# A recurrence with an early expert: weight loads issued one per half step behind a small GpSimd copy, masks moved to chunk 16, VectorE's splits put off

## The chip, the core and the metric

The kernel runs on one core of a Trainium2 chip. The metric is the device time of one execution in microseconds (us). Five engines take part: PE (TensorE, with PEld for its weight loads), ACT (ScalarE), DVE (VectorE), POOL (GpSimd) and SP (SyncE, which only issues DMAs). Each has a queue of its own that it works through in order; semaphores tie the queues together. In the profile, q1 is the DMA queue that SyncE and ScalarE feed, q0 the one that GpSimd feeds; both are served by the same 16 DMA engines.

## What is computed

A delta-rule attention without softmax over 768 tokens (4 batches, 8 heads, head size 48), and then a top-1 mixture of 8 experts on its 3072 output rows of 384 columns.

```python
k_n = k / (norm(k) + 1e-6)
for t in range(768):
    y[t]  = q[t] @ state
    v_old = k_n[t] @ state
    state = state + beta[t] * outer(k_n[t], v[t] - v_old)
x = y.reshape(3072, 384)                       # rows (batch, token)
e = argmax(x @ w_gate); gate = softmax(x @ w_gate)[e]
# each expert takes its rows in order, up to a capacity of 768
out[row] = gate * (relu(x[row] @ w1[e]) @ w2[e])
```

## The kernel before

**The recurrence.** The 768 tokens are cut into 24 chunks of 32. Inside a chunk the dependence between tokens is solved beforehand into a small triangular matrix T (`prepare` and `solve`, on VectorE, done by chunk 16), so that chunk c needs, for each half g of the heads (g = 0, 1), these steps in a row:

- `product_k` (line 326, TensorE): k times the state, into the tile ks in PSUM;
- `residual` (line 336, VectorE): R = vs - ks, where vs is v scaled by the norms (`tokens`, line 300, VectorE, for chunk c + 2 at the end of chunk c);
- `update` (lines 347 and 354): u = T times R on TensorE, and four copies of u, 32 partitions each, from PSUM into the tile u in SBUF;
- `state` (lines 367 and 375): the state s grows by k times u on TensorE, and four copies bring it from PSUM into the tile x, from which the next chunk's `product_k` reads.

The two halves run interleaved, so that a chunk is two half steps (c,0) and (c,1). Between them stand the output y of the chunk (lines 383 and 392, copied into xt at line 518, the last one at line 570), its store to xbuf in DRAM, and the logits of the router. `turn` (line 319) loads T for the next chunk as four DMAs of 32 KB from SyncE's queue. The score products P of a chunk pair are masked once on VectorE; `flush` (line 156) issues the masks that are ready, one pair ahead.

**Sharing.** From chunk `SHARED` = 18 on, the second half of the state copies goes to VectorE (line 375), and the router's and the early expert's work is done in the loop itself: after each `update`, `rt.step(budget=630)` issues one stage of the router's chain of small VectorE operations (`route`), `extra` splits weights of the early expert, `grab` issues the gathers of its rows once these are known. In the three half steps of `PARTED` two of the four copies of u are VectorE's as well.

**The early expert.** Expert number 0 in the order of processing is the one that has most rows after chunk 15 (`order`, line 895; its index is the tile widx). Its weights come by five indirect DMAs from GpSimd (`Experts.load`, line 1197): three of 512 KB for w1, two of 768 KB for w2. `LDS` says how many are issued at the head of a chunk: two in chunk 19, one each in 20 to 22. A weight is then split into a high part hw (a rounding copy on ScalarE, line 1056) and a low part lw = rw - hw (line 1057): by GpSimd for w1, by VectorE from chunk 22 on. `PCS` gives the number of these splits per half step; what is left follows behind the loop. The gathered rows are transposed in chunks 21 and 22 (`Experts.turn`, line 972) and split in the same way into x0h and x0l (lines 973 and 974).

**What sets the order.** In the loop the order on every engine is the order in which the code is written. The experts behind it are put in order by a scheduler.

The lines that issue the early weights and the splits:

```python
for _ in range(LDS.get(c, 0)):
    self.ahead.load()
```

## Time and profile before

| what | us |
|---|---|
| median of three executions | 514.58 (514.39 to 516.59) |
| the profiled execution, its own time | 516.29 |
| its span, first to last instruction | 514.5 |

| engine | busy us | share of the span | instructions |
|---|---|---|---|
| PE | 433.9 | 84% | 7404 |
| PEld | 373.3 | 73% | 7404 |
| DVE | 321.0 | 62% | 1043 |
| ACT | 281.1 | 55% | 784 |
| POOL | 121.7 | 24% | 122 |

The shares are means over stages. The recurrence takes about the first half of the span, the experts the second; chunks 16 to 23 lie between 193 and 257 us. In a timeline row stand the start, the duration, the engine, the line, the operation with the tile it writes and those it reads, the shape and how many instructions were merged; in brackets at the end, how long the engine was idle before and who released it ("issue" means that the trace names nobody).

### The profile page before, as it was taken

How to read it: one execution, taken by the hardware profiler on the slowest of the kernel's cores; microseconds unless marked ns; L12 is line 12 of the kernel's file. 1: busy time of each engine (PE TensorE's matmuls, PEld its weight loads, DVE VectorE, ACT ScalarE, POOL GpSimd, SP SyncE). 2: the span in 40 equal slices, each digit the busy share in tenths (PEclk: the TensorE clock that was granted, in tenths of full speed). 3: DMA queues.
4: the chain of work that ended last, by engine and by line, in shares of the span. 5: the costliest groups of instructions: out<-in, count | busy, mean ns of one | idle time of the engine just before them, and what ended most of it. 6: DMA issues, size and time to landing. Idle time of an engine off the chain costs nothing. (4 is left out here: it accounts for less than half of the span.)

```text
span 514.5 us, 17642 instructions
## 1 busy us (share of the span) xinstructions
PE 433.9 (84%) x7404; PEld 373.3 (73%) x7404; DVE 321.0 (62%) x1043; ACT 281.1 (55%) x784; POOL 121.7 (24%) x122
## 2 busy tenths in 40 slices
PE   5835766678888989957799899999999999999990
PEld 3424555456666666745589888999999999999990
DVE  1999699697999993747685736263360817263210
ACT  2237567687778888836652635273562818363210
POOL 6011000000000000226026453434253453521110
PEclk9885678798889999979999999999999999999996
DMA  5977223563335445557118274525144453610000
GB/s 154 236 233 200 60 79 84 175 173 84 91 86 180 103 114 148 152 147 195 44 46 294 90 244 141 164 89 199 72 162 170 154 186 89 205 72 31 29 32 14
DMA packets 49705, 67.17 MB, mean 131 GB/s; under 512 B 29084, under 2 KB 38230, under 8 KB 49619
## 3 DMA queue, kind: packets, MB, share of 16 engines
q0 software_dynamic: 9280, 34.98, 20.4%
q1 hardware_dynamic: 37570, 23.52, 17.8%
q10 hardware_dynamic: 2768, 7.47, 5.2%
q8 instruction: 60, 0.98, 0.8%
q14 instruction: 27, 0.21, 0.1%
HBM read 53.50 MB, written 12.43 MB: 128 GB/s over the span
## 5 line engine op out<-in xcount | busy, mean ns | idle before, releaser
L1098 DVE SCALAR_TENSOR_TENSOR hl<-hp,hh 128x256 fp32r<-128x256 f32 (+7 forms) x64 | 35.5, 554 | 92.1 <-ACT hh L1097 91.8
L1197 POOL DMA_INDIRECT rw<-in_w_dram,widx x40 | 40.9, 1022 | 143.5 <-DVE R L336 115.0
L354 ACT COPY u<-u 32x192 f32<-32x192 f32 x186 | 57.5, 309 | 22.2 <-PE u L347 17.8
L375 ACT COPY x<-s 48x192 f32<-48x192 f32 x164 | 51.3, 313 | 24.3 <-PE s L367 20.0
L1057 DVE TENSOR_TENSOR lw<-rw,hw 128x384 fp32r<-128x384 f32 (+1 forms) x106 | 59.6, 605 | 6.3 <-ACT hw L1056 6.3
L1095 PE MATMUL hp<-xh,hw 128*128 128x444 f32 (+6 forms) x168 | 58.9, 353 | 0.0
L1095 PE MATMUL hp<-xh,lw 128*128 128x444 f32 (+6 forms) x168 | 58.0, 345 | 0.0
L1095 PE MATMUL hp<-xl,hw 128*128 128x444 f32 (+6 forms) x168 | 58.0, 345 | 0.0
L1056 ACT CAST hw<-rw 128x384 fp32r<-128x384 f32 (+1 forms) x112 | 56.5, 557 | 0.1
L240 DVE TENSOR_TENSOR tmp<-M,AT 128x28 f32<-128x28 f32 (+23 forms) x180 | 55.8, 333 | 0.2
L245 DVE TENSOR_TENSOR M<-M,tmp 128x28 f32<-128x28 f32 (+23 forms) x180 | 55.8, 333 | 0.1
L347 PE MATMUL u<-R,T 128*64 128x48 f32 x736 | 35.2, 236 | 23.9 <-DVE R L336 14.4
L1097 ACT ACTIVATE hh<-hp 128x256 fp32r<-128x256 f32 (+7 forms) x64 | 31.3, 490 | 41.2 <-PE hp L1095 40.7
L1139 POOL DMA_INDIRECT out_dram<-ys,dst_row x27 | 29.1, 1078 | 101.6 <-ACT ys L1138 59.9
L347 PEld LDWEIGHTS u<-R,T 128*64 128x64 f32 x736 | 29.0, 147 | 32.7 <-DVE R L336 20.4
L132 PE MATMUL gp<-kq 48*32 48x64 f32 (+1 forms) x1792 | 27.4, 252 | 15.6 <-ACT P L152 6.7
L367 PE MATMUL s<-u,k 64*48 64x96 f32 x736 | 35.2, 271 | 4.6 <-ACT u L354 2.9
L132 PEld LDWEIGHTS gp<-kq 48*32 48x32 f32 x1792 | 21.9, 127 | 22.9 <-issue 8.5
L1115 PE MATMUL yT<-hh,hw 128*128 128x444 f32 (+3 forms) x96 | 34.2, 360 | 0.0
L1115 PE MATMUL yT<-hh,lw 128*128 128x444 f32 (+3 forms) x96 | 33.7, 354 | 0.0
L1115 PE MATMUL yT<-hl,hw 128*128 128x444 f32 (+3 forms) x96 | 33.4, 357 | 0.0
L367 PEld LDWEIGHTS s<-u,k 64*48 64x48 f32 x736 | 21.5, 129 | 15.4 <-ACT u L354 8.5
(219 smaller groups left out, 932.8 us busy)
## 6 DMA issues: line engine op xcount, KB each, us to landing
kq<-in_kqf_dram ACTq DMA_DIRECT2D x12, 448.0 KB
xbuf<-xt SPq DMA_DIRECT2D x24, 192.0 KB
v<-in_vt_dram SPq DMA_DIRECT2D x22, 192.0 KB
k<-in_kt_dram SPq DMA_DIRECT2D x21, 192.0 KB
kq<-in_kqf_dram SPq DMA_DIRECT2D x8, 448.0 KB
mb<-M SPq DMA_DIRECT2D x5, 512.0 KB
T<-mb SPq DMA_DIRECT2D x80, 32.0 KB
kq<-in_kqf_dram SPq DMA_DIRECT2D x4, 224.0 KB
```

Of the source, the lines that this page charges most:

```text
L132: nc.tensor.matmul(gp[a][32 * r : 32 * r + 32, i, t], kq[rows, 0, 4 * t + r], kq[rows, k0:k1, 4 * t + r], start=True, stop=True,)
L240: nc.vector.tensor_tensor(tv, M[:, :, r0:r1, j : j + 1].to_broadcast([128, G, m, n]), AT[:, :, j : j + 1, 32 - n : 32].to_broadcast([128, ...
L245: return lambda: nc.vector.tensor_tensor(v, v, tv, ALU.add)
L347: nc.tensor.matmul(us[p][64 * p : 64 * p + 64, m], T[:, 4 * g + m, 2 * p : 2 * p + 2].rearrange("p a b -> p (a b)"), R[:, m], start=True, ...
L354: copy(U[32 * r : 32 * r + 32, 4 * g : 4 * g + 4, r], us[r // 2][32 * r : 32 * r + 32])
L367: nc.tensor.matmul(self.S[h][64 * a : 64 * a + 48, t], kt[rows, m], U[rows, m, 2 * h : 2 * h + 2], start=first, stop=True, skip_group_chec ...
L375: copy(Xn[rows, ts, 2 * h : 2 * h + 2, a], self.S[h][rows, ts])
L1056: (nc.scalar.copy if e else self.hi)(hi[p], raw[p])
L1057: (nc.vector.tensor_tensor if e else self.lo)(lo[p], raw[p], hi[p], ALU.subtract)
L1095: nc.tensor.matmul(hp, a, b, start=i == 0, stop=i == len(terms) - 1)
L1115: self.nc.tensor.matmul(yT[m], a, b, start=j == 0, stop=j == len(terms) - 1)
L1197: nc.gpsimd.indirect_dma_start(out=raw[:, i * st : i * st + st].rearrange("p k m -> p (k m)"), out_offset=None, in_=tab[:, :], in_offset=b ...
```

## The change

- **Loads.** `LDS` is now a list of five half steps, (19,0), (19,1), (20,0), (20,1) and (21,1). Behind the `update` of each, GpSimd first copies one column of that half step's u into a tile of one column, z, and then issues one load. The copy waits for u, and GpSimd's queue behind it waits too.
- **A new function** `behind` does what followed the update from chunk `SHARED` on: work put off (`pay`), one stage of the router, the load, `grab`, `extra`. The gathers of `grab` now stand ahead of the splits of `extra`.
- **Splits.** In (20,0), (20,1), (21,0) one, two and three splits of w1 are done instead of two each.
- **VectorE's splits put off.** The low parts that VectorE computes in chunks 21 to 23 (x0l, and lw of w2) are kept in a list, `owed`, and issued by `pay` behind the next update.
- **Masks.** In chunk 16 `flush` is called for the last chunk, so that the three masks left are issued there; those of chunks 17, 19 and 21 go.
- **Sharing.** `SHARED` is 17, and in every half step from there on VectorE has one of the four copies of u (two in `PARTED`, as before).

```diff
-LDS = {19: 2, 20: 1, 21: 1, 22: 1}
-PCS = {(20, 0): 2, (20, 1): 2, (21, 0): 2, (22, 0): 1, (23, 0): 1}
+LDS = ((19, 0), (19, 1), (20, 0), (20, 1), (21, 1))
+PCS = {(20, 0): 1, (20, 1): 2, (21, 0): 3, (22, 0): 1, (23, 0): 1}
...
-SHARED = 18
+SHARED = 17
...
-            copy = nc.vector.tensor_copy if (c, g) in PARTED and r > 1 else nc.scalar.copy
+            copy = nc.vector.tensor_copy if c >= SHARED and r > 2 - ((c, g) in PARTED) else nc.scalar.copy
...
     def extra(self, c, i):
-        self.ahead.step(PCS.get((c, i), 0), self.nc.scalar.copy, self.nc.vector.tensor_tensor if c > 21 else None)
+        self.ahead.step(PCS.get((c, i), 0), self.nc.scalar.copy, self.defer if c > 21 else None)
+
+    def defer(self, *args):
+        self.owed.append(args)
+
+    def pay(self):
+        for args in self.owed:
+            self.nc.vector.tensor_tensor(*args)
+        self.owed = []
+
+    def behind(self, c, g):
+
+        self.pay()
+        self.rt.step(budget=630)
+        if (c, g) in LDS:
+            self.nc.gpsimd.tensor_copy(self.z, self.u[c % 2][:, 4 * g, 0, 0:1])
+            self.ahead.load()
+        self.grab(c)
+        self.extra(c, g)
...
-            for _ in range(LDS.get(c, 0)):
-                self.ahead.load()
...
-            self.flush(c)
+            self.flush(c if c < 16 else KC)
...
             if c >= SHARED:
-                rt.step(budget=630)
-                self.extra(c, 0)
-                self.grab(c)
+                self.behind(c, 0)
...
-                self.ahead.turn(c - KC + 3, self.ps)
+                self.ahead.turn(c - KC + 3, self.ps, lo=self.defer)
...
         rt.step()
+        self.pay()
         self.product_p(KC - 1)
...
         nc.scalar.copy(xh, tp)
-        nc.vector.tensor_tensor(xl, tp, xh, ALU.subtract)
+        (lo or nc.vector.tensor_tensor)(xl, tp, xh, ALU.subtract)
```

The second half step calls `behind(c, 1)` in the same way. The order on the engines, before and after, at three places:

GpSimd from the first load of the early expert's weights on, before (rw is the loaded weight, xg the gathered rows):

```order
L1197 DMA rw_4621<-in_w_dram,widx_75 128x1024 x3
L1057 TENSOR_TENSOR lw_4837<-rw_4621,hw_4836 128x512 x2
L963 DMA xg_4842<-xbuf,src_86 128x384 x2
L1057 TENSOR_TENSOR lw_4837<-rw_4621,hw_4836 128x512 x2
L1197 DMA rw_4942<-in_w_dram,widx_75 128x1536
L1057 TENSOR_TENSOR lw_4837<-rw_4621,hw_4836 128x512 x2
L1197 DMA rw_4942<-in_w_dram,widx_75 128x1536
```

GpSimd at the same place, after:

```order
L451 COPY z<-u_105 128x1
L1211 DMA rw_4674<-in_w_dram,widx_75 128x1024
L451 COPY z<-u_105 128x1
L1211 DMA rw_4674<-in_w_dram,widx_75 128x1024
L451 COPY z<-u_104 128x1
L1211 DMA rw_4674<-in_w_dram,widx_75 128x1024
L977 DMA xg_4842<-xbuf,src_86 128x384 x2
L1071 TENSOR_TENSOR lw_4846<-rw_4674,hw_4845 128x512
L451 COPY z<-u_104 128x1
L1211 DMA rw_4911<-in_w_dram,widx_75 128x1536
L1071 TENSOR_TENSOR lw_4846<-rw_4674,hw_4845 128x512 x5
L451 COPY z<-u_105 128x1
```

The three loads of w1 stand apart, each behind a copy; the gathers have moved ahead of all six split products, of which five now stand in one piece.

VectorE from the state copies in half step (21,1) to R of (22,0), before (sm, wv, ex and Eb are the first stage of the router):

```order
L375 COPY x_102<-s_951 48x2x2x48 x2
L698 TENSOR_REDUCE sm<-lg 128x4
L700 TENSOR_TENSOR wv<-lg,sm 128x32
L702 TENSOR_TENSOR wv<-wv,con 128x32
L704 TENSOR_REDUCE sm<-wv 128x4
L706 TENSOR_TENSOR ex<-lg,sm 128x32
L708 TENSOR_TENSOR Eb<-wv,sm 128x32
L974 TENSOR_TENSOR x0l<-tp,x0h 128x384
L300 TENSOR_TENSOR vs<-v,nt 128x384
L336 TENSOR_TENSOR R<-vs,ks 128x192
```

VectorE at the same place, after:

```order
L376 COPY x_102<-s_951 48x2x2x48 x2
L355 COPY u_105<-u 32x4x48
L712 TENSOR_REDUCE sm<-lg 128x4
L714 TENSOR_TENSOR wv<-lg,sm 128x32
L716 TENSOR_TENSOR wv<-wv,con 128x32
L718 TENSOR_REDUCE sm<-wv 128x4
L720 TENSOR_TENSOR ex<-lg,sm 128x32
L722 TENSOR_TENSOR Eb<-wv,sm 128x32
L301 TENSOR_TENSOR vs<-v,nt 128x384
L337 TENSOR_TENSOR R<-vs,ks 128x192
```

A copy of u has come in ahead of the router's stage, and x0l has left its place ahead of vs and R.

VectorE between R of (22,0) and R of (22,1), before:

```order
L336 TENSOR_TENSOR R<-vs,ks 128x192
L375 COPY x_102<-s_951 48x2x2x48 x2
L724 TENSOR_REDUCE sum<-Eb 128x8
L726 TENSOR_TENSOR pe<-Eb,pp 128x32
L728 TENSOR_TENSOR run<-run,sum 128x8
L730 TENSOR_TENSOR V<-Eb,con 128x4x24
L1057 TENSOR_TENSOR lw_5145<-rw_4942,hw_5144 128x384
L336 TENSOR_TENSOR R<-vs,ks 128x192
```

And after:

```order
L337 TENSOR_TENSOR R<-vs,ks 128x192
L376 COPY x_102<-s_951 48x2x2x48 x2
L355 COPY u_104<-u 32x4x48
L443 TENSOR_TENSOR x0l<-tp,x0h 128x384
L738 TENSOR_REDUCE sum<-Eb 128x8
L740 TENSOR_TENSOR pe<-Eb,pp 128x32
L742 TENSOR_TENSOR run<-run,sum 128x8
L744 TENSOR_TENSOR V<-Eb,con 128x4x24
L337 TENSOR_TENSOR R<-vs,ks 128x192
```

The split of w2 (lw) has gone from its place ahead of R to behind the next update, and x0l of chunk 21 stands here instead, behind the copy of u.

## Rows read from the trace of the kernel before

**Rows 1.** Windows: stretch, length, busy us per engine, granted PE clock, DMA share, GB/s.

```profile
core 0: us, PE busy (x) PEld busy (x) DVE busy (x) ACT busy (x) POOL busy (x), PEclk, DMA share, GB/s
...
218.00:226.00 8.00, 2.61 (x59) 2.07 (x50) 1.78 (x5) 1.50 (x5) 0.00 (x0) 0.75 0.77 225
...
258.00:514.00 256.00, 240.33 (x1480) 230.89 (x1479) 114.52 (x266) 112.40 (x243) 92.81 (x92) 0.98 0.37 125
```

**Rows 2.** Timeline: R(18,0), R(19,0), R(20,0), R(20,1) and the u copies behind it.

```profile
205.76 0.35 DVE L336 TENSOR_TENSOR R<-vs,ks 128x192 f32<-128x192 f32 x1 [0.81 <-PE ks L326]
...
212.57 0.35 DVE L336 TENSOR_TENSOR R<-vs,ks 128x192 f32<-128x192 f32 x1
...
218.44 0.35 DVE L336 TENSOR_TENSOR R<-vs,ks 128x192 f32<-128x192 f32 x1
...
229.42 0.34 DVE L336 TENSOR_TENSOR R<-vs,ks 128x192 f32<-128x192 f32 x1
...
230.63 0.75 DVE L354 COPY u<-u 32x192 f32<-32x192 f32 x2 [0.23 <-PE u L347]
```

**Rows 3.** Timeline: the update's matmuls in half step (20,0).

```profile
222.96 0.42 PE L347 MATMUL u<-R,T 128*64 128x48 f32 x2 [4.17 <-issue]
...
224.59 1.06 PE L347 MATMUL u<-R,T 128*64 128x48 f32 x14 [1.22 <-DMA T<-mb]
```

**Rows 4.** Timeline: the first of three weight loads, and T for chunk 20.

```profile
213.09 1.45 POOL L1197 DMA_INDIRECT rw<-in_w_dram,widx  x1 [115.03 <-DVE R L336]
...
213.47 3.53 SPq L319 DMA_DIRECT2D T<-mb  x4
```

**Rows 5.** DMA queues from 216 to 218 us: packets, MB, share of 16 engines.

```profile
q0 software_dynamic: 145, 0.54, 106.7%
q1 hardware_dynamic: 57, 0.02, 4.8%
```

**Rows 6.** Timeline: VectorE and GpSimd in chunks 20 and 21, with one mask before.

```profile
199.33 0.68 DVE L148 TENSOR_TENSOR P<-P,mask 128x512 f32<-128x512 f32 x1
...
226.47 0.35 DVE L767 TENSOR_TENSOR acc<-acc,ip 128x192 f32<-128x192 f32 x1
...
226.99 2.49 POOL L1057 TENSOR_TENSOR lw<-rw,hw 128x512 fp32r<-128x512 f32 x2 [9.95 <-ACT hw L1056]
227.07 1.22 DVE L780 TENSOR_TENSOR o<-o,top 128x16 f32<-128x16 f32 x1
...
228.53 0.98 DVE L771 CAST src<-of 128x2 int32<-128x2 f32 x1
...
230.27 0.97 POOL L963 DMA_INDIRECT xg<-xbuf,src  x1 [0.79 <-issue]
...
231.41 0.56 DVE L300 TENSOR_TENSOR vs<-v,nt 128x384 f32<-128x384 f32 x1
...
232.57 3.30 DVE L148 TENSOR_TENSOR P<-P,mask 128x512 f32<-128x512 f32 x1
...
232.81 2.50 POOL L1057 TENSOR_TENSOR lw<-rw,hw 128x512 fp32r<-128x512 f32 x2
...
235.47 1.24 POOL L1197 DMA_INDIRECT rw<-in_w_dram,widx  x1 [0.16 <-issue]
```

**Rows 7.** Timeline: R(16,1).

```profile
195.70 0.35 DVE L336 TENSOR_TENSOR R<-vs,ks 128x192 f32<-128x192 f32 x1 [1.38 <-PE ks L326]
```

**Rows 8.** Timeline: R(22,0), ks, a split, R(22,1), R(23,0), the last xt.

```profile
241.94 0.35 DVE L336 TENSOR_TENSOR R<-vs,ks 128x192 f32<-128x192 f32 x1
...
244.09 0.56 PE L326 MATMUL ks<-x,kq 112*32 112x96 f32 x16
...
245.10 0.56 DVE L1057 TENSOR_TENSOR lw<-rw,hw 128x384 fp32r<-128x384 f32 x1 [1.33 <-ACT hw L1056]
...
245.57 0.35 DVE L336 TENSOR_TENSOR R<-vs,ks 128x192 f32<-128x192 f32 x1
...
249.63 0.34 DVE L336 TENSOR_TENSOR R<-vs,ks 128x192 f32<-128x192 f32 x1
...
257.28 0.48 ACT L570 COPY xt<-y 128x384 f32<-128x384 f32 x1 [1.06 <-PE y L392]
```

More of the change, by code (lines that the diff above doesn't have):

```diff
@@ L434, in extra @@
     def extra(self, c, i):
-        self.ahead.step(PCS.get((c, i), 0), self.nc.scalar.copy, self.nc.vector.tensor_tensor if c > 21 else None)
+        self.ahead.step(PCS.get((c, i), 0), self.nc.scalar.copy, self.defer if c > 21 else None)
[4 more added lines that the diff above has]
+            self.nc.vector.tensor_tensor(*args)
+        self.owed = []
+    def behind(self, c, g):
[6 more added lines that the diff above has]
+        self.extra(c, g)
     def grab(self, c):
@@ L539, in run_ @@
                 if c >= SHARED:
-                    rt.step(budget=630)
-                    self.extra(c, 1)
-                    self.grab(c)
+                    self.behind(c, 1)
                 self.maybe(c + 1)
@@ L966, in collect, with turn @@
             )
-    def turn(self, i, ps, tag="gp"):
+    def turn(self, i, ps, tag="gp", lo=None):
         nc, xg, (xh, xl) = self.nc, self.xg[:, i], [x[:, i] for x in self.x]
```

## The prediction

> **What bounds the kernel now.** I read first where TensorE, the engine with the most work, is not working. From 258 us to the end it is busy for 240.33 of 256 us [rows 1]; what the change can shorten lies ahead of that, in the recurrence over 24 chunks. There a chunk goes through TensorE, ScalarE and VectorE and back, one half of the heads after the other; I write R(c,g) for the subtraction of VectorE (line 336) that opens half step g of chunk c. R(23,1) is the last of them, and the others are counted back from it. Where all runs well a chunk takes 5.87 us, from R(19,0) to R(20,0), and half a chunk 2.94 [rows 2]. Then two places stick out.
>
> The first is the update of chunk 20. R(20,0) starts at 218.44, but its matmuls wait 4.17 us and then 1.22 more, the second time plainly for the loads of T; they end at 225.65 (224.59 + 1.06), where in the next half step they are done 1.2 us after R (R at 229.42, the copies of their result at 230.63), which here is 219.65: 6.0 us lost [rows 2, 3]. Those four loads of T start at 213.47 on SyncE's queue (q1), beside three loads of the early expert's weights that GpSimd issues from 213.09 on (q0) [rows 4]. From 216 to 218 q0 takes 106.7% of the sixteen engines and q1 4.8% [rows 5]. So the weights hold T back. TensorE, idle so long, has a mean granted clock of 0.75 in that stretch [rows 1], between its two levels, and stays slow a little longer: from the end of the late matmuls to R(20,1) it takes 3.77 us instead of the 1.7 that remain of a half step (2.94 less 1.2): 2.0 us more [rows 2, 3].
>
> The second is VectorE against GpSimd. A mask product that takes 0.68 us alone takes 3.30 at 232.57, beside two products of GpSimd (2.50 us for both), and all that stands behind it on VectorE is 2.6 us late [rows 6]. A small one with both operands in SBUF suffers alike: 16 columns take 1.22 us from 227.07, to just past the end of the first of two GpSimd products that began at 226.99 [rows 6].
>
> **The change part by part**, from R(20,0) = 0 where it matters.
>
> Chunks 16 to 19. Three masks in one place put 3 x 0.68 = 2.04 us on VectorE in chunk 16, against 1.38 us of idle time before R(16,1) [rows 6, 7]; with what else stands there I take 0.4 us lost. Chunks 17 and 18 hand two of four state copies and one of four u copies per half step from ScalarE to VectorE; chunk 18 takes 6.81 us now and 19, where the state copies are shared already, 5.87 [rows 2]. Of 0.94 too much in chunk 18, and as much in 17, I take 1.3 us as won. But the u copy stands ahead of the routing operations on VectorE, and the next R waits behind these in chunks 18 and 19: up to 0.37 us (half of the 0.75 for two [rows 2]) three times, less a mask of 0.68 gone from (19,0); 0.4 us lost. Sum: 0.5 us won, between 1.1 lost and 1.8 won.
>
> Chunks 20 and 21: before, 241.94 - 218.44 = 23.50 us from R(20,0) to R(22,0) [rows 2, 8]. Each weight load now waits on GpSimd for the u of its half step, so load 1 follows u(19,0). A load's data fills the engines 2 to 3 us after its issue (213.09, full by 216) and for some 2 us (0.54 MB of q0 from 216 to 218, where a load is 0.52 MB) [rows 4, 5], so T for chunk 20, issued 0.9 us after R(19,0), is through before load 1. Loads 2 and 3 fall around T for chunk 21, issued at +0.8 and wanted at about +6.4; with 2 us lost to load 2 and a part of that to load 3 it just makes it. Without waits R(22,0) would come at 2 x 5.87 plus about 0.8 for ScalarE's casts: +12.5, a gain of 11.0.
>
> I do not take that, because of the order on GpSimd. Behind the third load now stand the two gathers of the expert's rows, and behind these all six split products. The gathers need the source rows: VectorE's u copies end 1.96 after R (230.63 + 0.75 - 229.42) [rows 2]; the five small operations from acc to the cast took 3.04 (226.47 to 229.51), of which some 1.85 lie in two that GpSimd held, so 1.2; the gather follows 0.76 after the cast (230.27): +3.9. Two gathers take 2.54 (to the product at 232.81): +6.5. The first product, 1.25: +7.7. The fourth load with its small copy, 1.24 and 0.16 (235.31 to 235.47) and 0.2 taken for the copy (no row has it; between 0 and a product's 1.25): +9.3. Five products in a row, 6.25: +15.55 [rows 6]. The casts they need are done on ScalarE by +10. In this train fall, on VectorE, four small products of the routing step of (21,1), from about +11, and then the v scaling (vs, 0.56 alone), all with both operands in SBUF, and R(22,0) stands behind them. Let each small one pass where a GpSimd product ends, and vs at the train's end: R(22,0) at +16.1. If VectorE is held through the whole train, as the mask was through two, the routing's small ones (0.9 for these) follow it too: +17.0; if nothing is held, +12.5. I take 16.1, since the small product of 1.22 us passed at an end and the large mask did not. TensorE then idles some 4 us, and its clock may fall as it did after 6; half of the 2.0 us above: 1.0. Gain: 23.50 - 16.1 - 1.0 = 6.4.
>
> The Trainium skill says of this place (SBUF — State Buffer, Who interferes with whom) that a VectorE instruction with two SBUF inputs contends with a GpSimd instruction that reads SBUF, and whoever issues second is fully blocked. The 3.30 us agree, though the mask, which waited, could by it have passed between the two products. By the rule R(22,0) comes at +16.1, by the mask's row at +17.0.
>
> Chunk 22. A split of VectorE stands ahead of each next R and waits for ScalarE, 1.33 us at 245.10; R(22,1) starts at 245.57 though ks was done at 244.65 (244.09 + 0.56): 0.92 late [rows 8]. Put off by half a step, the splits stand behind the u copy and wait for nothing. I take 0.9 for the first half and, since VectorE's own queue (u copy, split, routing) is then near its limit, 0.5 for the second: 6.3 us where 7.69 stand (241.94 to 249.63), 1.4 won, between 0.5 and 1.8.
>
> Chunk 23 to the last copy xt: 7.65 us now. In (23,1) u copy and split (0.37, 0.56) now stand ahead of the last routing, which waited for TensorE before; against it a split less ahead of R(23,1). I take 0.2 lost, between 0.5 lost and 0.5 won.
>
> From there, 257.2 us remain (514.50 - 257.28), and the chain (last routing, weights of the next expert, gathers) moves as a whole. The order of the first experts differs: four gathers now go ahead of two output scatters, and TensorE transposes all four in a piece. The gathers start earlier by the scatter that stood ahead, the transposes need the last of the four sooner: nothing, within 1.0 either way. Loads 4 and 5 arrive long before the products of expert 0.
>
> **Sum:** 0.5 + 6.4 + 1.4 - 0.2 = 8.1 us. The profiled execution took 516.29 (span 514.50), 1.71 above the median of 514.58; no row says where, so I take the 8.1 from the median: **506.5 us**.
>
> **The rivals.**
> - *GpSimd's train holds nobody.* For: the rows show VectorE held beside two products, none beside five, and whether its small ones slip between is seen once. Against: the long rows above. Gain 0.5 + 11.0 + 1.4 - 0.2 = 12.7: 501.9. Chance 0.22.
> - *The wait for T moves to chunk 21*, held by loads 2 and 3 as chunk 20's was by three. It ends when load 3 is in; then the routing of (21,1) falls behind the train and is not held. With the 6.0 us and the clock's 2.0, R(22,0) at 12.5 + 8.0 = +20.5, gain 3.0 + 1.7 = 4.7: 509.9. For: q1's 4.8%; against: two loads, not three, and about a microsecond without either between them. Chance 0.12.
> - *The weights were not what held T.* For: the longer wait (4.17) has no releaser named. The Trainium skill (DMA: Bandwidth & Descriptors, Queues, rings and completion order) has each engine go round its queues packet by packet, by which q1 would have kept a share; the 4.8% speak against it. If something else held T, the 6.0 us stay and 8.1 - 6.0 = 2.1 are left: 512.5, no difference. Chance 0.07.
> - *Slower: every T meets a load.* With one load per half step, T for chunks 21, 22 and 23 each run into one (loads 2 and 3, 4, 5). If each waits as chunk 20's did, 3 x 6.0 = 18 us go back against the best case: 501.9 + 18 = 519.9. It decides from the point where a load holds q1 for the 5.6 us between T's issue and its use; three loads did, one filled the engines for 2. Chance 0.04.
>
> **How the numbers follow.** My forecast has 0.55. About 0.5% (2.6 us) is what a measurement of this kernel can tell from no change, so faster means below 512.0: 0.55 + 0.22 + 0.12, less a little for their tails: 0.88; within: 0.08; slower: 0.04. The range reaches down to the first rival with chunks 16 to 19 at their better end (501.0) and up past the second with them at the worse (511.0).
>
> **What would show it.** In the changed kernel's trace: no wait at the update of chunk 20; GpSimd's five products in one piece, with VectorE's wv, ex, Eb and vs beside it at a microsecond or more each; 16 to 17 us from R(20,0) to R(22,0), then 6.3 to R(23,0); the stretch after the last xt within 1 us of 257.2. If the second distance is near 12.5, the train was harmless; if the wait sits at chunk 21's update, the loads still collide.

## The result, and the profile after

The changed kernel takes 521.06 us (median, 520.55 to 523.01), the kernel before beside it 514.91: a ratio of 1.0109, 95% interval 1.0076 to 1.0141. It is slower, by some 6 us. The forecast was 506.5 us with a range of 501.0 to 511.0, and slower had a chance of 0.04.

The profiled execution took 521.12 us, its span is 519.3 us. The openings of the half steps on VectorE, R(18,0), R(19,0), R(20,0), R(20,1), R(22,0) and R(23,0), and the last xt on ScalarE, as in [rows 2, 8]:

```profile
205.56 0.35 DVE L337 TENSOR_TENSOR R<-vs,ks 128x192 f32<-128x192 f32 x1
...
213.69 0.34 DVE L337 TENSOR_TENSOR R<-vs,ks 128x192 f32<-128x192 f32 x1
...
221.95 0.35 DVE L337 TENSOR_TENSOR R<-vs,ks 128x192 f32<-128x192 f32 x1
...
228.91 0.35 DVE L337 TENSOR_TENSOR R<-vs,ks 128x192 f32<-128x192 f32 x1 [3.65 <-remote]
...
241.18 0.35 DVE L337 TENSOR_TENSOR R<-vs,ks 128x192 f32<-128x192 f32 x1 [0.28 <-PE s L368]
...
249.69 0.35 DVE L337 TENSOR_TENSOR R<-vs,ks 128x192 f32<-128x192 f32 x1
...
259.54 0.48 ACT L584 COPY xt<-y 128x384 f32<-128x384 f32 x1 [1.06 <-PE y L393]
```

Cut at such rows, the two spans differ so:

| stretch | before, us | changed, us |
|---|---|---|
| start to R(16,0) | 193.17 | 191.26 |
| chunks 16 to 19 | 25.27 | 30.69 |
| chunks 20 and 21 | 23.50 | 19.23 |
| chunk 22 | 7.69 | 8.51 |
| chunk 23 to the last xt | 7.65 | 9.85 |
| from there to the end | 257.2 | 259.8 |

Chunks 20 and 21, the aim of the change, gain 4.3 us. Everything around them loses. Chunk 18 goes from 6.81 to 8.13 us, chunk 19 from 5.87 to 8.26, with neither loads nor splits in the first of them. What a half step there waits for, in the timeline of (18,1), ScalarE and VectorE:

```profile
210.69 0.97 ACT L355 COPY u<-u 32x192 f32<-32x192 f32 x3
...
211.70 0.36 DVE L355 COPY u<-u 32x192 f32<-32x192 f32 x1 [0.97 <-ACT u L355]
...
213.22 0.55 DVE L301 TENSOR_TENSOR vs<-v,nt 128x384 f32<-128x384 f32 x1
213.69 0.34 DVE L337 TENSOR_TENSOR R<-vs,ks 128x192 f32<-128x192 f32 x1
```

VectorE's one copy of u does not run beside ScalarE's three. It starts when the last of them is done and ends at 212.06, where four copies on ScalarE would have ended too. Behind it stand the router's operations, vs and the next R; R has no bracket, so it came straight off a full queue. A bracket of that kind (0.97 to 2.98 us idle, ended by ScalarE's u) stands at each of the eleven half steps from (17,0) on that are not in `PARTED`; about 1 us of it are ScalarE's three copies. Inside, the two pairs run side by side:

```profile
223.20 0.64 ACT L355 COPY u<-u 32x192 f32<-32x192 f32 x2 [1.13 <-PE u L348]
223.28 0.75 DVE L355 COPY u<-u 32x192 f32<-32x192 f32 x2 [0.35 <-PE u L348]
```

The code says which tiles these are. The result of `update` lies in two PSUM tiles, `us[r // 2]`. In `PARTED` ScalarE reads the first and VectorE the second, and TensorE releases both (the brackets above). With one copy for VectorE, quarter 2 goes to ScalarE and quarter 3 to VectorE from the *same* tile, and in the trace it is ScalarE's third copy, done at 211.66, that releases VectorE's. The tile u that both write in SBUF can't be the reason, since they write it side by side in `PARTED`.

The Trainium skill (PSUM — Partial Sum Buffer, PSUM bank collisions raise a hardware error) has two engines collide in one bank where they touch the same 32 partitions, and not where they touch different ones, as these quarters do. The program waits all the same; no run here tried it without.

### The profile page after: what moved, and what is told of

It is laid out like the page before. It is cut to its first block, busy times and chain, and to the rows that moved or that the text cites. A ratio compares the mean times of both kernels' runs of the same rounds, so it can differ in the third digit from the quotient of the medians.

```text
span 519.3 us, 17641 instructions
## 1 busy us (share of the span) xinstructions
PE 436.0 (84%) x7400; PEld 376.2 (72%) x7404; DVE 322.5 (62%) x1058; ACT 276.9 (53%) x769; POOL 121.2 (23%) x127
## 5 line engine op out<-in xcount | busy, mean ns | idle before, releaser
L376 ACT COPY x<-s 48x192 f32<-48x192 f32 x160 | 50.0, 313 | 29.1 <-PE s L368 22.6
L355 ACT COPY u<-u 32x192 f32<-32x192 f32 x175 | 54.1, 309 | 20.9 <-PE u L348 17.1
L1071 DVE TENSOR_TENSOR lw<-rw,hw 128x384 fp32r<-128x384 f32 (+1 forms) x104 | 58.4, 605 | 1.9 <-ACT hw L1070 1.8
L368 PE MATMUL s<-u,k 64*48 64x96 f32 x736 | 33.5, 269 | 4.2 <-ACT u L355 2.1
L327 PE MATMUL ks<-x,kq 112*32 112x96 f32 x736 | 29.0, 272 | 5.3 <-issue 5.3
```

Of the source, the lines that this page charges most:

```text
L355: copy(U[32 * r : 32 * r + 32, 4 * g : 4 * g + 4, r], us[r // 2][32 * r : 32 * r + 32])
L376: copy(Xn[rows, ts, 2 * h : 2 * h + 2, a], self.S[h][rows, ts])
L1071: (nc.vector.tensor_tensor if e else self.lo)(lo[p], raw[p], hi[p], ALU.subtract)
```

## Experiments

Every ratio is taken against runs of the kernel before on the same chip. e1 to e8 ran on one chip (the kernel before: 511.35 and 511.22 us there), e9 to e12 and f1 to f4 on a second (515.22 and 516.10), f5 and f6 on a third (515.08); the chip of the result above is not on record. Stretches in us are read from one profiled execution each, at the rows named above. Executions of one kernel lie up to 8 us apart (e4: 512.28 to 520.34), so a difference of a stretch counts where several kernels show it or a row shows the wait.

| kernel | ratio, 95% interval | 16 to 19 | 20 and 21 | 22 | 23 | behind xt |
|---|---|---|---|---|---|---|
| before | 1 | 25.27 | 23.50 | 7.69 | 7.65 | 257.2 |
| changed, again (e11) | 1.0146, 1.0096 to 1.0196 | 32.19 | 19.33 | 10.18 | 9.86 | 261.4 |
| e1, third quarter | 0.9879, 0.9812 to 0.9946 | 25.89 | 17.01 | 6.49 | 7.88 | 254.6 |
| e2, u as before | 0.9872, 0.9795 to 0.9948 | 25.02 | 18.53 | 8.03 | 7.69 | 255.4 |
| e3, two of four | 0.9966, 0.9928 to 1.0004 | 26.95 | 16.53 | 8.01 | 8.63 | 254.9 |
| e4, before + u copy | 1.0078, 1.0032 to 1.0123 | 30.76 | 17.68 | 8.19 | 9.99 | 255.0 |
| e5, before + pacing | 0.9944, 0.9910 to 0.9977 | 25.19 | 19.66 | 8.13 | 7.65 | 254.5 |
| e6, before + put off | 0.9956, 0.9916 to 0.9996 | 25.27 | 23.15 | 6.67 | 7.69 | 256.3 |
| e7, before + masks, 17 | 0.9938, 0.9898 to 0.9978 | 24.52 | 21.72 | 8.11 | 7.65 | 255.4 |
| e8, e1 + three T | 0.9938, 0.9903 to 0.9973 | 26.59 | 16.56 | 8.26 | 7.87 | 254.6 |
| e9, e1 + short train | 0.9949, 0.9918 to 0.9979 | 26.41 | 17.65 | 6.61 | 9.18 | 258.1 |
| e10, e8 + short train | 1.0000, 0.9972 to 1.0028 | 30.28 | 17.70 | 6.61 | 9.18 | 259.1 |
| e12, before + three T | 0.9984, 0.9949 to 1.0019 | 28.13 | 18.78 | 7.69 | 7.65 | 260.4 |
| f4, e9 + late loads | 0.9938, 0.9910 to 0.9967 | 26.36 | 18.86 | 6.61 | 9.18 | 259.2 |
| f5, f4 + late gathers | 1.0059, 1.0022 to 1.0096 | 26.58 | 21.05 | 7.72 | 9.19 | 260.2 |
| f6, e1 + late gathers | 0.9955, 0.9921 to 0.9988 | 26.64 | 17.76 | 6.50 | 7.87 | 259.4 |

### The copy of u

**e1: VectorE takes the third quarter, ScalarE the fourth.** The same number of copies on each engine; now VectorE's comes first on the shared tile.

```diff
-... c >= SHARED and r > 2 - ((c, g) in PARTED) ...
+... c >= SHARED and r in ((2, 3) if (c, g) in PARTED else (2,)) ...
```

> The changed kernel, only that VectorE copies the third quarter of u and ScalarE the fourth (the number of copies on each engine is the same). In the changed kernel the copy of VectorE starts 1 to 1.9 us late, since ScalarE reads the same PSUM tile ahead of it. Theory A (this wait is the loss): without it VectorE's queue, the router's stages and the next R come about 1 us sooner in most half steps; chunks 17 to 19 go from 8.1 to 8.3 us down to 6 to 6.9, chunk 22 from 8.5 to about 7, chunk 23 from 9.9 to about 8, together 6 to 9 us: 512 to 515. Rival B (VectorE simply has too much work with a copy of u in each half step, whoever it waits for): no more than 2 us back, 519 to 521. Rival C (the loss lies in the loads, the gathers and the order of the experts behind the recurrence): chunks 17 to 19 may shrink, but the time stays above 518.

Measured 0.9879, where the changed kernel itself has 1.0146 (e11; 1.0109 in the result): 2.3 to 2.7%, 12 to 14 us, between them. In the timeline of (18,1) VectorE's copy starts with ScalarE's first:

```profile
209.44 0.35 DVE L355 COPY u<-u 32x192 f32<-32x192 f32 x1
209.48 0.98 ACT L355 COPY u<-u 32x192 f32<-32x192 f32 x3
211.42 0.35 DVE L337 TENSOR_TENSOR R<-vs,ks 128x192 f32<-128x192 f32 x1
```

From the copy's start to R it is 1.98 us, as in the changed kernel (211.70 to 213.69: 1.99): the same work, a microsecond sooner. Only the order on the tile was changed. Against the first profile of the changed kernel e1 wins 4.8 us in chunks 16 to 19, 2.0 in chunk 22 and 2.0 in chunk 23, where these rows stand: 8.8 us, within theory A's 6 to 9. There the wait is the loss. The 2.2 us in chunks 20 and 21 and the 5 behind the last xt came along and have no such row; how far they belong to the edit is open (below).

**e2: copies of u as before, the rest as changed.**

```diff
-... c >= SHARED and r > 2 - ((c, g) in PARTED) ...
+... (c, g) in PARTED and r > 1 ...
```

> The changed kernel with the copies of u as before (two on VectorE in PARTED, none elsewhere); everything else as changed. Theory A (the wait of VectorE's single copy is the loss): all of it comes back, chunks 18 and 19 at 5.9 to 6.8 us, chunk 22 at 7 and 23 at 8: 510 to 514. Rival B (too much work on VectorE): the same here. Rival C (loads, gathers, order of the experts): it stays at 518 to 521.

Measured 0.9872, like e1. Sharing u outside `PARTED` brings nothing that shows, even where it does not wait.

**e3: two of the four copies on VectorE from chunk 17 on.**

```diff
-... c >= SHARED and r > 2 - ((c, g) in PARTED) ...
+... c >= SHARED and r > 1 ...
```

> The changed kernel with two of the four copies of u on VectorE in every half step from chunk 17 on, as PARTED has them, so that each engine reads a PSUM tile of its own. Theory A (the wait is the loss): no copy waits for the other engine's, u is ready some 0.7 us earlier per half step: 508 to 514. Rival B (too much work on VectorE): with one copy more per half step it gets worse than the changed kernel, 521 to 526. Rival C: 517 to 521.

Measured 0.9966. No copy waits for the other engine, and it is still a little slower than e1 (509.84 against 505.34 us on the same chip): chunk 19 takes 7.17 us, 22 and 23 take 8.01 and 8.63, where e1 has 6.27, 6.49 and 7.88. So rival B has a part: 0.37 us more of VectorE per half step costs too, but far less than the wait.

**e4: the kernel before, with VectorE on the last quarter from chunk 18 on.**

```diff
-... (c, g) in PARTED and r > 1 ...
+... c >= SHARED and r > 2 - ((c, g) in PARTED) ...
```

> The kernel before with one edit: from chunk 18 on VectorE makes the last of the four copies of u, as in the changed kernel. Theory A (the wait): chunks 18 and 19 go from 6.8 and 5.9 us to 8.1 and 8.3, chunks 22 and 23 get longer by 1 to 2 us each: 520 to 523. Rival B (work on VectorE): 517 to 520, as there is a copy of 0.37 us more per half step. Rival C (loads, gathers, experts): as before, 514 to 516.

Measured 1.0078, some 4 us: less than theory A had, and by the time alone within rival B's range. The wait itself stands in its rows:

```profile
205.84 0.97 ACT L354 COPY u<-u 32x192 f32<-32x192 f32 x3
206.84 0.36 DVE L354 COPY u<-u 32x192 f32<-32x192 f32 x1 [3.03 <-ACT u L354]
```

Chunks 18 and 19 lose 5.5 us (9.81 and 8.37 us), but chunk 20 gives 5.7 back: it takes 8.14 us instead of 13.86, since its update waits for R alone. The first of the three weight loads and that update:

```profile
213.83 1.41 POOL L1197 DMA_INDIRECT rw<-in_w_dram,widx  x1 [118.82 <-ACT x L375]
...
222.05 0.98 PE L347 MATMUL u<-R,T 128*64 128x48 f32 x16 [1.52 <-DVE R L336]
```

The fault alone looks small in this kernel because another wait hides it; with that wait removed, in the changed kernel, it is paid in full.

### The other parts, one by one

**e5: loads, copies z, gathers ahead of splits, and `PCS`, in the kernel before.**

```diff
+LDS = ((19, 0), (19, 1), (20, 0), (20, 1), (21, 1))
+PCS = {(20, 0): 1, (20, 1): 2, (21, 0): 3, (22, 0): 1, (23, 0): 1}
...
+                self.behind(c, 0)
```

> The kernel before with the loads, the small GpSimd copies, the new order of gathers and splits and the new PCS alone (SHARED 18, copies of u, masks and VectorE's splits as before). Theory P (all that the changed kernel gains once the copy of u no longer waits comes from the pacing): 20.00 to 18.5 us or less from R(20,0) to R(22,0) where 23.50 stood, 5 to 7 us faster than the kernel before. Rival Q (the gain needs the deferred splits and the masks too): 2 to 4 us faster. Rival T (T still meets a load, now in another half step, for as long as before): within 1 us of the kernel before.

Measured 0.9944, 2.9 us, as rival Q had it; chunks 20 and 21 give 3.8. The wait for T is shorter, not gone: at the update of chunk 20 the matmuls wait 0.80 us, with no releaser named, and then 1.31 us for T. e2 shows it too:

```profile
218.43 0.29 PE L348 MATMUL u<-R,T 128*64 128x48 f32 x2 [0.82 <-DVE R L337]
219.98 0.64 PE L348 MATMUL u<-R,T 128*64 128x48 f32 x14 [1.26 <-DMA T<-mb]
```

**e6: VectorE's splits put off, in the kernel before.**

```diff
-self.nc.vector.tensor_tensor if c > 21 else None
+self.defer if c > 21 else None
...
-self.ahead.turn(c - KC + 3, self.ps)
+self.ahead.turn(c - KC + 3, self.ps, lo=self.defer)
```

> The kernel before with VectorE's splits of chunks 21 to 23 put off behind the next update, and nothing else. By the recorded steps chunk 22 gets 1.4 us shorter (7.69 to 6.3) and chunk 23 0.2 longer: 1.2 us faster. Rival: the split only changes its place and holds the router's stage behind it, chunk 22 stays at 7.5 to 8: no change, within 0.5 us.

Measured 0.9956, 2.2 us (0.2 to 4.3). Chunk 22 falls from 7.69 to 6.67, chunk 23 goes from 7.65 to 7.69: 1.0 us where the steps had 1.2.

**e7: `SHARED` 17 and the three masks in chunk 16, in the kernel before.**

```diff
-SHARED = 18
+SHARED = 17
...
-            self.flush(c)
+            self.flush(c if c < 16 else KC)
```

> The kernel before with SHARED 17 and with the three last masks issued in chunk 16, copies of u as before, and nothing else. By the recorded steps: 1.3 us won in chunks 17 and 18 by the sharing, 0.4 lost in chunk 16; beyond these the mask of 3.30 us that stood beside GpSimd's products in chunk 21 is gone, which can give up to 2.6 us where T for chunk 20 is still late. 0.9 to 3.5 us faster. Rival: what VectorE gains there is waited for at the update of chunk 20, whose T comes when the loads are through: no change.

Measured 0.9938, 3.2 us. Chunk 16 loses 0.65 (6.54), chunks 17 and 18 win 1.32 together (6.44 and 5.75), chunk 21, from which the mask of 3.30 us [rows 6] is gone, wins 1.7 (7.96), and chunk 22 gives 0.4 of that back. The mask's place beside GpSimd was worth as much as the sharing.

### GpSimd's train, and three tiles for T

In the changed kernel the train did not hold VectorE: the copy of u waited longer. GpSimd's last three products, then VectorE's copy and the router's first product:

```profile
235.84 3.73 POOL L1071 TENSOR_TENSOR lw<-rw,hw 128x512 fp32r<-128x512 f32 x3 [0.87 <-ACT hw L1070]
...
238.94 0.36 DVE L355 COPY u<-u 32x192 f32<-32x192 f32 x1 [1.85 <-ACT u L355]
...
239.55 0.20 DVE L714 TENSOR_TENSOR wv<-lg,sm 128x32 f32<-128x32 f32 x1
```

In e1, without that wait, it does: wv takes 1.55 us and ends at 233.06, with the train (226.84 + 6.16 = 233.00).

```profile
226.84 6.16 POOL L1071 TENSOR_TENSOR lw<-rw,hw 128x512 fp32r<-128x512 f32 x5
...
231.51 1.55 DVE L714 TENSOR_TENSOR wv<-lg,sm 128x32 f32<-128x32 f32 x1
```

**e8: e1 with three tiles for T, each loaded a chunk earlier** (R gets two buffers to make room).

```diff
-self.T = [... for i in range(2)]
+self.T = [... for i in range(3)]
...
                 self.maybe(c + 1)
+            if c > 16:
+                self.maybe(c + 2)
```

> The changed kernel with VectorE on the third quarter of u (which removes the wait for ScalarE), and with three tiles for T instead of two, so that from chunk 17 on T is loaded a chunk earlier (one tile for R fewer makes the room). Theory T (a load still holds T for 1 to 2 us at the update of chunk 20 or 21): R(20,0) to R(22,0) falls from 17.0 to 14.5 to 16 us, 1 to 3 us faster than with two tiles. Rival G (GpSimd's five products hold VectorE's router stage, and R(22,0) comes when they end): the wait for T goes, the distance stays at 16 to 17 us and the time within 1 us.

The wait for T at (21,0) is gone: that half step takes 3.09 us instead of 5.13. The train takes it all back. wv now stands 3.79 us, to the train's end (228.01 + 6.18 = 234.19), and (21,1) takes 7.26 us instead of 5.66:

```profile
228.01 6.18 POOL L1073 TENSOR_TENSOR lw<-rw,hw 128x512 fp32r<-128x512 f32 x5
...
230.46 3.79 DVE L716 TENSOR_TENSOR wv<-lg,sm 128x32 f32<-128x32 f32 x1
```

Rival G holds. The Trainium skill's rule on VectorE and GpSimd, weighed in the prediction (SBUF — State Buffer, Who interferes with whom), is borne out in that the second engine is fully blocked. Whether it can pass between two products of GpSimd that follow one another stays open: wv did not in e1, e2, e3, e5 and e8 (1.55, 3.11, 3.47, 3.11 and 3.79 us, each to the piece's end), but the small product o of [rows 6] did, and again in e4, e6, e7 and e12 (1.22 to 1.27 us, done with the first of two products). What decides between the two no run shows.

**e9 and e10: e1 and e8 with three split products on GpSimd, the other three put off on VectorE.**

```diff
-PCS = {(20, 0): 1, (20, 1): 2, (21, 0): 3, (22, 0): 1, (23, 0): 1}
+PCS = {(20, 0): 1, (20, 1): 2, (22, 0): 1, (22, 1): 1, (23, 0): 2, (23, 1): 1}
```

> The changed kernel with VectorE on the third quarter of u (no wait for ScalarE), and with three split products on GpSimd instead of six: after the fourth load only two follow in one piece; the other three splits of w1, and two of w2 as before, go to VectorE in chunks 22 and 23, put off like the others. Theory G (a VectorE product with both operands in SBUF stands still until GpSimd's piece of products ends): wv of the router's stage takes 0.2 us instead of 1.55, R(22,0) follows R(21,1) after 3.5 to 4.5 us instead of 5.66; chunks 22 and 23 lose 0.5 to 1.5 us to the added splits: 0 to 2 us faster than with six. Rival V (the router's stage is not what R(22,0) waits for): the distance stays at 5.7 and the time is 0.5 to 1.5 us longer.

> The same with three tiles for T, loaded a chunk earlier. Theory G: with T there in time, wv took 3.79 us there and R(22,0) came 7.26 us after R(21,1); with two products in the piece wv takes 0.2 to 1 us and the distance is 3 to 4.5 us, chunks 20 and 21 together 12.3 to 14 instead of 16.56; of the 3 to 4 us won 0.5 to 1.5 are lost again in chunks 22 and 23: 504 to 506, the fastest of all. Rival V: 16 us and more for chunks 20 and 21, 507 to 510.

The mechanism is as said: wv takes 0.19 us behind a piece that ends at 229.21, and (21,1) takes 3.76 and 3.75 us.

```profile
226.71 2.50 POOL L1071 TENSOR_TENSOR lw<-rw,hw 128x512 fp32r<-128x512 f32 x2
...
231.90 0.19 DVE L714 TENSOR_TENSOR wv<-lg,sm 128x32 f32<-128x32 f32 x1
```

The times are not: 0.9949 and 1.0000, and chunks 20 and 21 as long as ever, since (20,0) now takes 7.1 us in both, with TensorE in pieces (below). Chunk 23 loses 1.3 to the added splits.

**e12: three tiles for T in the kernel before, nothing else.** (The diff of e8.)

> The kernel before with three tiles for T and with T loaded a chunk earlier from chunk 17 on, nothing else: what the wait for T alone is worth. By the recorded steps the update of chunk 20 loses 6.0 us to it and the clock 2.0 more: R(20,0) to R(22,0) from 23.50 to about 15.5, 6 to 8 us faster. Rival X (the long wait at that update, 4.17 us without a named releaser, isn't for T): 0 to 2 us faster. Rival Y (VectorE and GpSimd then meet earlier, and the router's products and a mask wait for the split products): 2 to 5 us faster.

Measured 0.9984: no difference, as rival X had it by the time. Chunks 20 and 21 give 4.7 us. (20,0) still takes 4.97, and not for TensorE: ks is done at 221.45, but VectorE's o and then the cast stand 1.27 and 0.98 us beside two products of GpSimd, and R(20,1) comes straight behind them. That is what rival Y had:

```profile
220.94 0.51 PE L326 MATMUL ks<-x,kq 112*32 112x96 f32 x15
...
222.33 0.98 DVE L773 CAST src<-of 128x2 int32<-128x2 f32 x1
223.22 0.34 DVE L336 TENSOR_TENSOR R<-vs,ks 128x192 f32<-128x192 f32 x1
```

Chunks 18 and 19 (7.78 and 7.74) and the stretch behind xt lose it again; in e10 the two chunks take 8.43 and 8.95, in e8 7.45 and 6.24. In all three kernels vs of chunk 19, with R(19,0) behind it, waits for the transfer of v (0.88, 1.90 and 1.28 us in e12, e10 and e8), which it does neither before nor in e1. By what the earlier loads of T delay v was not followed up. T alone was not worth the 8.0 us of the steps.

### Where TensorE stops

**e11: the changed kernel once more.**

> The changed kernel itself once more, beside the others. Theory K (the stretch behind the last xt is longer there, 259.8 us against 254.5 to 255.4 in the kernels without the wait, because TensorE leaves the recurrence at a lower granted clock: 0.77 to 0.89 in the first 30 us): the same again, clock below 0.9 in these 30 us and over 258 us. Rival L (it was that one execution): a clock of 1.0 and 254.5 to 256 us, and the whole 1.5 to 2.5% slower than the version with the third quarter all the same, from chunks 17 to 23. The ratio to the kernel before should stay at 1.005 to 1.015.

1.0146, 261.4 us behind the last xt, and a mean granted clock of 0.66, 1.00 and 0.83 in the three windows of 10 us from there: the numbers of theory K. Its reason is another matter. The windows in the first run of the changed kernel, then in e1 (columns as in [rows 1]):

```profile
259.54:269.54 10.00, 9.52 (x109) 9.09 (x102) 8.23 (x47) 4.33 (x13) 1.25 (x2) 0.83 0.08 22
269.54:279.54 10.00, 7.11 (x92) 6.80 (x91) 5.66 (x24) 2.28 (x6) 6.12 (x7) 0.89 0.75 234
279.54:289.54 10.00, 10.00 (x52) 9.96 (x52) 3.83 (x14) 1.77 (x4) 5.34 (x6) 0.77 0.62 211
```

```profile
249.07:259.07 10.00, 8.74 (x113) 8.24 (x106) 8.53 (x51) 4.43 (x14) 1.72 (x2) 1.00 0.12 30
259.07:269.07 10.00, 10.00 (x114) 9.80 (x113) 8.23 (x29) 2.63 (x8) 6.10 (x7) 1.00 0.77 246
269.07:279.07 10.00, 8.93 (x63) 8.46 (x62) 3.17 (x9) 6.30 (x16) 5.84 (x6) 1.00 0.60 213
```

The changed kernel's TensorE comes out of the recurrence with 5.74 us busy in the last 10 (e1: 8.21), and its mean granted clock in the 30 us behind is 0.83, 0.89 and 0.77, between its two levels, where e1 stays at the upper one. But f6 (below) leaves the recurrence with e1's 8.21 us and has 0.83, 0.90 and 0.76 all the same, with 259.4 us behind xt. The window ahead of its last xt, and the one behind:

```profile
241.68:251.68 10.00, 8.21 (x252) 6.38 (x244) 7.99 (x35) 6.03 (x19) 0.00 (x0) 1.00 0.16 43
251.68:261.68 10.00, 9.52 (x109) 9.10 (x102) 8.24 (x48) 4.34 (x13) 1.26 (x2) 0.83 0.08 22
```

So theory K's reason is not shown. What the long kernels share is the second window: there TensorE is busy for 6.0 to 7.1 of 10 us in the changed kernel, e9 to e12 and f1 to f6 (258.1 to 261.4 us behind xt), and for 10.00 in before and e1 to e8 (254.5 to 257.2). These groups are also chips: e1 to e8 ran on one, e9 to f6 on two others, and no kernel is on record as profiled on chips of both groups. So this stretch may differ by the chip, and what e1 wins there against the changed kernel is not shown to come from the edit.

In the second window the changed kernel's TensorE is idle for 2.9 us, in the midst of 56 small matmuls that e1 runs in one piece:

```profile
273.90 0.97 PE L950 MATMUL ip<-V,A 128*128 128x8 bf16 x32
276.91 0.19 DVE L888 TENSOR_TENSOR w<-w,ip 128x32 f32<-128x32 f32 x1 [3.21 <-remote]
277.15 0.58 PE L950 MATMUL ip<-V,A 128*128 128x8 bf16 x17 [2.29 <-issue]
278.33 0.34 PE L950 MATMUL ip<-V,A 128*128 128x8 bf16 x7 [0.60 <-issue]
```

No releaser is named ahead of the 17, but they come just behind VectorE's w (in e11 the same row names w), and w stood 3.21 us for sums that TensorE's rows show as done at 274.87; "remote" means that no instruction in the profile raised the semaphore at that moment. (20,0) of the changed kernel has the same: VectorE is idle for 3.65 us ahead of R(20,1) ("remote"), though ks and s are recorded as done by 226.92, and TensorE then waits for R.

```profile
226.37 0.55 PE L368 MATMUL s<-u,k 64*48 64x96 f32 x16
...
229.32 0.88 PE L348 MATMUL u<-R,T 128*64 128x48 f32 x16 [2.40 <-DVE R L337]
```

So the stops of TensorE are in part stands of the engines that wait for its semaphore. In e9 TensorE's own rows fall into pieces of a few matmuls:

```profile
220.19 0.53 PE L368 MATMUL s<-u,k 64*48 64x96 f32 x10
...
220.99 0.39 PE L368 MATMUL s<-u,k 64*48 64x96 f32 x4 [0.27 <-issue]
...
221.76 0.35 PE L368 MATMUL s<-u,k 64*48 64x96 f32 x2 [0.38 <-issue]
```

**f1, f2, f3: 64 unused matmuls of one column at the start** of the changed kernel, of e1 and of the kernel before. They move TensorE's later instructions against the transfers that bring them.

```diff
             self.nc.tensor.matmul(wp, self.warm[:, 0:128], self.warm, start=True, stop=True)
+        for _ in range(64 if tag == "y" and n == 4 else 0):
+            self.nc.tensor.matmul(wp[:, 0:1], self.warm[:, 0:128], self.warm[:, 0:1], start=True, stop=True)
```

> The changed kernel with 64 matmuls of one column more at the very start of TensorE's program (128 more instructions with their weight loads; the result of these is not used). It moves every later instruction of TensorE by half of the 256 instructions that one transfer of 16 KB on its instruction queue (q8) holds, and changes nothing else. In the changed kernel TensorE stops in half step (20,1), from 226.9 to 228.9 us, with no releaser named, and starts again just as such a transfer is through, beside the third load of weights; it stops once more some 15 us behind the last xt. Theory I (TensorE has run out of instructions, whose transfer stands behind the weights): both stops move to another place or go, and the time changes by 1 to 5 us either way. Rival S (a semaphore or the loads themselves hold it): R(20,0) to R(20,1) stays at 6 to 7 us and the stretch behind xt at 259 to 262 us; the time is that of the changed kernel, within 1 us but for some 3 us at the start.

> The same 64 matmuls ahead of the version with VectorE on the third quarter of u, which shows neither stop (R(20,0) to R(20,1) 3.24 us, 254.6 us behind the last xt). Theory I: with the boundary elsewhere a stop of 1 to 4 us can come up in chunks 20 and 21 or behind xt, always with no releaser named and ended by a transfer on q8. Rival S: no stop appears; the same time but for the start.

> The same 64 matmuls ahead of the kernel before. There TensorE waits 4.17 us at the update of chunk 20 with no releaser named, until a q8 transfer is in, and 1.22 us more for T. Theory I: the first wait changes or goes, and what is left is the wait for T alone (up to the same moment, if T is the later of the two: then R(20,1) comes no earlier and only the name of the releaser changes). Rival S: 4.17 and 1.22 us as before.

The ratios are 1.0288, 1.0173 and 1.0186; the start itself costs some 12 us (R(16,0) at 203.6 to 205.0), so only stretches count. f1: (20,0) 6.11 us and 260.0 behind xt, as rival S has it. f2: (20,0) goes from 3.24 to 5.40, and 259.0 stand behind xt where e1, on another chip, had 254.6: a stop has come up. f3: the wait of 4.17 us is gone, (20,0) takes 3.82 instead of 10.98, but (19,0) takes 5.31 where before had 2.91, with TensorE in pieces of 3, 4, 4 and 5 matmuls. One of three speaks for rival S: not settled by these. The first weight load and the update of chunk 20 in f3, which waits neither for a load nor for T:

```profile
224.92 1.44 POOL L1199 DMA_INDIRECT rw<-in_w_dram,widx  x1 [115.11 <-DVE R L338]
...
233.00 0.74 PE L349 MATMUL u<-R,T 128*64 128x48 f32 x16
```

**f4: e9 with the third and fourth load a half step later. f5: f4 with the gathers a half step later too. f6: e1 with the late gathers.**

```diff
-LDS = ((19, 0), (19, 1), (20, 0), (20, 1), (21, 1))
+LDS = ((19, 0), (19, 1), (20, 1), (21, 0), (21, 1))      # f4, f5
...
-        if rt.full and (rt.late or c > CLOSE):
+        if rt.full and (rt.late or c > CLOSE) and c > 20:      # f5, f6
```

> The version with the third quarter and three split products on GpSimd (7.10 us from R(20,0) to R(20,1), most of it a stop of TensorE without a releaser beside the third load), with the third and the fourth load each one half step later, behind u of (20,1) and (21,0). Theory I: the third load no longer stands in the way of the transfer on q8, and the half step takes 3 to 3.5 us; the stop may come up a half step later. Rival S (something else in that half step stops TensorE): 6 to 7 us as before.

> The version before it (three split products on GpSimd, third and fourth load a half step later) with the two gathers of the early expert's rows also later, behind the update of (21,0) instead of (20,1). There TensorE worked through y in pieces (27, 4 and 1 matmuls) in half step (20,1), before the third load's data came but while the gathers were issued; R(20,1) to R(21,0) took 5.39 us. Theory J (what stops TensorE stands beside what GpSimd's queue q0 moves, gathers as much as loads): the pieces go from (20,1), 3 to 3.6 us there, and come up where the gathers are now, in (21,0) or (21,1). Rival I2 (TensorE stops at a fixed place of its program, where a transfer on q8 is due): the pieces stay in (20,1), at the same matmuls of y.

> The version with VectorE on the third quarter of u, all six split products on GpSimd, with the gathers of the rows behind the update of (21,0). The train of five products then falls apart into two and three with the fourth load and the gathers between, and the three end later against the router's stage of (21,1). Theory G (VectorE's products stand until GpSimd's piece ends): wv of that stage still waits for the last three, 1 to 3.5 us, so R(21,1) to R(22,0) stays at 5.5 to 7 us: the time within 2 us of 0.988 of the kernel before. Rival: the shorter piece lets it pass, 3.5 to 4.5 us there and 0.983.

f4: (20,0) falls from 7.10 to 3.24 us, and the stop comes up in (20,1), 5.39 us, beside the gathers. f5, on another chip: with the gathers gone from there (20,1) takes 3.67, and the stop stands where they are now, in (21,1), which takes 10.68, though 2.41 of these are TensorE's plain wait for the gathered rows (ahead of their transposes at 236.74):

```profile
228.81 0.35 PE L384 MATMUL y<-x,kq 112*32 112x96 f32 x3
229.03 0.97 POOL L977 DMA_INDIRECT xg<-xbuf,src  x1 [0.31 <-issue]
229.44 0.38 PE L384 MATMUL y<-x,kq 112*32 112x96 f32 x5 [0.27 <-issue]
230.30 0.96 POOL L977 DMA_INDIRECT xg<-xbuf,src  x1 [0.30 <-issue]
230.88 0.37 PE L384 MATMUL y<-x,kq 112*32 112x96 f32 x5 [1.06 <-issue]
...
232.32 1.17 PE L384 MATMUL y<-x,kq 112*32 112x96 f32 x18 [0.48 <-issue]
```

f6: (21,0), where its gathers are, takes 5.16 us; VectorE is idle for 3.22 of them ahead of R(21,1), again by "remote". wv stands 1.40 us, to the end of the last three products, as theory G has it; but (21,1) takes 4.33 us, the rival's distance, and the ratio of 0.9955 is neither's.

So what stands moves with what GpSimd issues, and not with a fixed place of TensorE's program. With the third load gone from (20,0) that half step runs through, though the gathers come 3.9 us behind R(20,0) as in e9 (4.0); with the gathers moved too, (20,1) runs through. Where an R was held beside the gathers (the changed kernel, e9, e10 and f6) it comes 0.6 to 0.9 us behind the end of the second gather's row (228.22, 222.44, 228.28 and 232.34). Beside weight loads alone TensorE works in pieces in (19,0) of f3 and e12. Each is one execution, and f5 and f6 ran on another chip than f4 and e1. By what path the stops reach TensorE, or the engines that wait for it, stays open: in f5 no transfer on the instruction queue q8 starts between 228 and 233 us, so the reading that TensorE waits for a late transfer of instructions is not shown. Not every gather brings one: e1, whose gathers stand in (20,1), has none of this length in (20,0) or (20,1).

## Why the prediction was wrong

The steps against the changed kernel and against e1, which has all of the change but the wait (gains in us, from the profiled executions):

| step | forecast | changed | e1 |
|---|---|---|---|
| chunks 16 to 19 | +0.5 | -5.4 | -0.6 |
| chunks 20 and 21 | +6.4 | +4.3 | +6.5 |
| chunk 22 | +1.4 | -0.8 | +1.2 |
| chunk 23 | -0.2 | -2.2 | -0.2 |
| behind the last xt | 0 | -2.6 | +2.6 |

**The step that failed** is the price of the copy of u: "up to 0.37 us (half of the 0.75 for two [rows 2]) three times". The row was one of `PARTED`, where VectorE reads a tile of its own. A single copy shares its tile with ScalarE's third and waits for it: about 1 us in each half step outside `PARTED`, from chunk 17 to 23, with the router, vs and R behind it. Chunks 16 to 19 lose 5.4 us by it, where 0.5 won was forecast. No rival had it. That e1, with the same number of copies on each engine, wins 8.8 us back in chunks 16 to 19, 22 and 23 shows it.

**Chunks 20 and 21.** The pacing does what was said at the update of chunk 20: in the changed kernel its 16 matmuls run in one piece and wait for R alone.

```profile
222.36 0.89 PE L348 MATMUL u<-R,T 128*64 128x48 f32 x16 [1.52 <-DVE R L337]
```

"T for chunk 20 [...] is through before load 1" held by that update there and in e1, not in e2 and e5, which still wait 1.3 us. The gain is 4.3 us and not 6.4: (20,0) takes 6.96 us, 3.65 of them VectorE's idle time ahead of R(20,1), which no step had. The 16.1 + 1.0 us that were forecast are 17.01 in e1, but not by the forecast's route. The choice that a small product passes between two of GpSimd, as o did [rows 6], was wrong for this one: wv stood to the train's end in e1, e2, e3, e5 and e8, as the mask had; the value of +17.0, which the text also gave, was the right one. That e1's wv was held for 1.55 us only comes from a wait for T (0.70) and a short stop (1.10) ahead of it.

**The wait of 4.17 us** [rows 3] was taken for T. e12 takes T's lateness away and gains nothing in the whole, and f3 loses the 4.17 by a shift of TensorE's program. The rival "The weights were not what held T" came nearest: a wait that names nobody is not the wait of the next row that does. T itself came in 11.5, 11.1 and 11.3 us after the first of the three loads was issued in before, e6 and e7, but it was there without a wait at the updates of e4 and f3, 8.2 and 8.1 us after it. So three loads beside T do not by themselves hold it for the 6.0 us; what added the rest is open. Nor are the 2.0 us more all the clock's: ks for R(20,1) is done at 228.81 (227.96 + 0.85), and R comes at 229.42, straight behind the cast that GpSimd held [rows 6], so 0.6 us of them are VectorE's.

**Chunks 16 to 19 without the wait.** e7 shows the terms: masks 0.65 lost (0.4 said), sharing 1.32 won (1.3 said).

**Chunk 22 and 23.** The deferral is worth 1.0 alone (e6) and 1.2 in e1, of 1.4 said, but chunk 22 takes 8.0 us and more in e2, e3 and e8, which have it too; chunk 23 is right in e1 (0.2 lost). In the changed kernel the copy's wait (1.18, 0.97, 1.19, 1.81) covers both.

**Behind the last xt** the bound was 1.0 either way. It lies between 254.5 and 261.4 us in these kernels, long where TensorE is idle in the second window; that was in no step, and the chip stands as a rival to every edit here.

The three parts alone gain 0.56, 0.44 and 0.62%, together 1.6% or 8.3 us, where 8.1 were forecast for the whole; in one kernel, without the copy's wait (e1, e2), they give 1.2 to 1.3%. That the sum comes near is partly luck: the pacing (e5) gave 2.9 us where its step had 6.4, masks and sharing (e7) 3.2 where 0.9 were said.

## What to carry to other kernels

Before work is moved to another engine, look at which tile the two engines then share: one copy fewer on ScalarE wins nothing if the other engine waits for its last, and giving away the copy that comes first on the tile instead of the last removes the wait at no cost. Take the price of a moved instruction from a row with the same neighbours and the same waits, not from one with the same shape. Try the parts of a change apart: a fault can hide behind a wait that another part removes, as in e4, and a wait removed can come back at the next engine, as in e8.

The fastest versions here are the changed kernel with the third quarter on VectorE (e1, 505.34 us) and with the copies of u as before (e2, 507.08), against 511.35 of the kernel before on that chip; the two can't be told apart.

## What was not expected of the hardware

- A product of 128x32 on VectorE, both operands in SBUF, stood 1.55, 3.11 and 3.79 us (e1, e2, e8), each time to the end of a piece of five GpSimd products, and took 0.19 us beside none; one of 128x16 stood 1.22 us and passed between two (before).
- For 2 to 4 us TensorE, or an engine that waits for its semaphore, stands without a releaser in the profile, TensorE often working on in pieces of 3 to 8 matmuls, while GpSimd issues gathers or loads; f4 and f5 move the stop by moving these.
- 64 matmuls of one column at the very start put R(16,0) off by some 12 us, where 3 were expected. They themselves take 1.89 us (f3); the first update then waits 17.95 us with no releaser named, where before waits 10.66 for GpSimd.
